# Attention inputs loaded ahead of weights, and two groups of heads side by side, in a fused attention and feed-forward kernel

## The chip, the cores and the metric

The kernel runs on one core of a Trainium2 chip. The time is the device time of one execution in microseconds (us); the profile of an execution gives its span, from the first to the last instruction. The engines are TensorE (PE, matmuls; PEld is its weight loads), VectorE (DVE), ScalarE (ACT) and GpSimd (POOL); SyncE (SP) issues most loads, POOL issues the others. Engines work in parallel, each through its own queue in order, and wait for one another through semaphores.

## The reference

```python
def sm_attn(qq, kk, vv):
    s = scale * np.matmul(qq, kk.transpose(0, 1, 3, 2))
    a = np.exp(s - np.max(s, axis=-1, keepdims=True))
    a = a / (np.sum(a, axis=-1, keepdims=True) + 1e-09)
    return np.matmul(a, vv)
p_packed = sm_attn(p, k, v)              # 32 packed queries against 576 keys
attn = sm_attn(q, p_packed, p_packed)    # 576 queries against the 32
x = attn.transpose(0, 2, 1, 3).reshape(8 * 576, 512)
h = x @ w_in                             # first feed-forward, 512 to 2048
x = (h * (1.0 / (1.0 + np.exp(-1.702 * h)))) @ w_out
h = np.maximum(np.maximum(x @ w1, x @ w2), x @ w3)   # second, 512 to 768
out = h @ w_out2
```

There are 8 batches of 8 heads, 576 tokens each, head size 64. The weights come as float64, the other inputs as float32.

## The kernel before

**Tiles and stages.** Attention works in 16 groups: a batch `b` and one of its two groups `g` of four heads. A group is a list of steps: `load_pk` (step 0), `load_v` (step 2) and `load_q` (step 7) issue its loads; `split_pk` builds a block-diagonal `pbd` from the packed queries; then s1 (packed queries times keys, `s`), a maximum (DVE), an exponential (ACT), transposes of the exponentials (`t` and `t1r`, copied to `et` by ACT), the product with v (`pv`), its masked and scaled copy (`pn`, DVE), its transpose (`ptp`, kept as `pt` and as a new `pbd`), s2 (queries times packed keys, also `s`), a softmax on DVE and ACT in the transposed layout (`a`), and `at`, the transposed probabilities, split by ACT and POOL.

The first feed-forward is folded with it: `pw` is packed value times `w_in`, so that `h` is `at` times `pw`. It goes chunk by chunk of 128 of the 2048 columns: `h_unit` (for two halves of 288 tokens), `g_unit` (the gate: `t` and `g`, on ACT, DVE, sometimes POOL) and `out_unit` (`acc`, with `w_out`). A product of two fp32 matrices is three matmuls of high and low parts (`mm3`). The second feed-forward follows from about 900 us on.

**Weights.** `w_in` and `w_out` arrive as the bits of float64. A piece of 1 MB (`raw_wi` or `raw_wo`, two loads of 512 KB on the SP queue) is turned into a high and a low part by `conv`: for the first four pieces by `convert`, six DVE instructions and two on ACT; for later ones by `convert_low`, which loads a second, shifted copy (`low_wi`, `low_wo`). Both piece kinds are named by quarter `n` of the 2048 columns: wi_0 is the pair for quarter 0. Converted `w_in` pieces are also saved to memory (`wsc`, by `wi_save`, 1 MB each, issued from POOL) for use by later batches.

**Order.** `main` makes a list of (due time, function) with `add`; the list is sorted by due time and traced in that order. The due times are plan numbers in us, not measured times. `attention(t, b, g, stretch)` gives step k of a group the time t plus its offset times `stretch`; `conv(t, ..., load, ...)` issues the loads `load` before t and the parts of the conversion at t and after it; `tn[n]` is the time of chunk n and starts at `T0`. The framework then orders each engine's queue, which runs strictly in that order. The SP queue has at most eight loads in flight: the ninth is issued when the first has landed.

Of the kernel before, what the change touches and what calls it, by code (L numbers as in the profile page):

```python
# [8 lines left out]
F32 = mybir.dt.float32  # L9
# [4 lines left out]
ALU = mybir.AluOpType  # L14
AX = mybir.AxisListType

B, H, S, D, NP = 8, 8, 576, 64, 32
DM, DFF, DFF2 = 512, 2048, 768
NT = B * S
P = 128  # L20
TB = 512
# [6 lines left out]
KD = DM // P  # L28
NQ = DFF // TB
SCALE = 1.0 / D ** 0.5  # L30
D_ = [-2, -8, 2.9, -2.51, 2.83, -0.47, -3.58, -0.6, 0.92, -0.32, -6.66, 0.91, 2.97, 2.32, -5.59, -0.32]
W_ = [60, 15.02, 42.09, 0]
K_ = [2, 11, -8, 6, 1, -7, 10, 6, -11, -14, -9, -5, -2, -13, -1, 4]
L_ = [8.18, 16.49, 4, 22.39]
Z_ = [1, 1, 1, 0, 0, 0, 0, 0, 0, 0, 0, 0, 0, 0, 0, 0]
PL_ = [10, 12]
Q_ = [12, 9, 9, 8]
# [5 lines left out]
def tile_packed_attention_moe(  # L43
# [13 lines left out]
    nc = tc.nc  # L57
# [5 lines left out]
    def stage_pool(name, bufs, side):  # L63
        return tc.alloc_tile_pool(name=name, bufs=bufs, side=side, reuse_waits="tile")
# [4 lines left out]
    ap_ = stage_pool("ap", 1, "right")  # L69
# [7 lines left out]
    def f(t):  # L77
        return t.bitcast(F32)
# [8 lines left out]
    def ur_tile(name):  # L87
        return urp.tile([P, S], F32, tag="ur", name=name)

    def u_tile(name, dt=F32):  # L90
        return up.tile([P, S], dt, tag="u", name=name)

    def x_tile(name, dt=F32):
        return up.tile([P, 4 * HALF], dt, tag="x", bufs=4, name=name)
# [24 lines left out]
    wsc = dram.tile([2, NQ, 2, P, 2, TB], F32R, name="wsc")  # L119

    wsa = dram.tile([9, P, 2, 2, 3, P], F32R, name="wsa")
    wss = dram.tile([9, P, 2, 2, 4, P], F32R, name="wss")


    def split(raw, hi, lo):
        nc.scalar.copy(hi, raw)  # L126
        nc.gpsimd.tensor_tensor(out=lo, in0=raw, in1=f(hi), op=ALU.subtract)  # L127

    def evac(o, hi, lo):
        nc.scalar.copy(hi, o)  # L130
# [67 lines left out]
    class Group:  # L198
# [2 lines left out]

        def load_pk(self):
            b, g = self.b, self.g
            self.praw = ap_.tile([P, 2, NP], F32, tag="praw", name=f"praw_{self.n}")
            nc.sync.dma_start(self.praw, p[b, g])
            self.kraw = self.load_t(k, "k")

# [33 lines left out]
        def split_t(self, raws, name):  # L241
            t = []
            for c in range(2):
                hl = [u_tile(f"{name}{x}_{self.n}_{c}", F32R) for x in range(2)]
                split(raws[c], *hl)
                t.append(hl)
            return t

        def load_v(self):
            self.vraw = []  # L250
            for c in range(3):
                raw = (u_tile if self.b < 2 else ur_tile)(f"raw_v_{self.n}_{c}")
                if c < 2:
                    nc.sync.dma_start(raw[:, :TB], v[self.b, self.g, :, c])
                else:
                    nc.sync.dma_start(raw[D:, :2 * P], vr[self.b, self.g])
                self.vraw.append(raw)

        def split_v(self):
            if self.b < 2:  # L260
                return
            self.v = []
            for c in range(3):
                if c < 2:
                    hl = [u_tile(f"v{x}_{self.n}_{c}", F32R) for x in range(2)]
                    split(self.vraw[c][:, :TB], *(t[:, :TB] for t in hl))
                else:
                    t = u_tile(f"v_{self.n}_{c}", F32R)
                    hl = [t[:, :2 * P], t[:, 2 * P:4 * P]]
                    split(self.vraw[c][D:, :2 * P], *(t[D:] for t in hl))  # L270
                self.v.append(hl)
# [205 lines left out]

    wo = {}
    gt, acc = {}, {}
    latest = {}  # L480

# [25 lines left out]
    start = {}  # L509
# [88 lines left out]
    class Piece:  # L598
# [12 lines left out]
        def conv(self):  # L611
            self.hl = [c_tile(f"wa{y}_{self.n}") for y in range(2)]
            self.v, self.s = conv_late(self.n, self.raw, *self.hl, TB)
# [211 lines left out]
    def add(t, fn, *a):  # L825
        plan.append((t, len(plan), fn, a))
# [27 lines left out]

    tpt, tend = {}, [0.0]

    def attention(t, b, g, stretch, dq=0.0):
        ts = []
        for k, (dt, fn) in enumerate(Group(b, g).steps()):
            after = {9: 7, 13: 12, 12: 11, 11: 10, 10: 8, 8: 6, 6: 5, 5: 3, 3: 1, 4: 2, 1: 0}.get(k)  # L860
            tk = t + dt * stretch + (D_[k] if b == 0 else 0) + (dq if k in (7, 9, 11, 12, 13) else 0)
            ts.append(tk if after is None else max(tk, ts[after] + .05))
            add(ts[-1], fn)
        tpt[b, g] = ts[10] + .05
        tend[0] = max(tend[0], ts[-1])

    def main():
        HU = 2.2
        T0 = 39

        attention(0.0, 0, 0, 1.07)
        attention(8, 0, 1, 1.07)
        attention(20, 1, 0, 0.97, 0)
        attention(34, 1, 1, 0.97, 0)

        N1 = 2 * B * NFC
        tn = [0.0] * 300
        t = T0
        for n in range(N1 + 2):
# [10 lines left out]
        sv = {}  # L890

        def wi_save(g, n):
            nc.gpsimd.dma_start(f(wsc[g, n].rearrange("c p a b -> p c a b")), f(sv[g, n]))

        def wi_store(g, n):
            def s(ws):
                sv[g, n] = ws
                if W_[n] == 0:
                    wi_save(g, n)
                for c in range(2):  # L900
                    wi[0, 2 * g + c, n] = ws[:, c]
            return s

        def wo_store(fc):
            def s(ws):
                wo[fc], wo[fc + 1] = (ws[:, x] for x in range(2))
            return s

        kk = 0
        for n in range(NQ):  # L910
            def tc_(kk):
                base = 7 + 6.49 * kk if n == 0 else tn[start[0, n]] - 22 + 7 * (kk - 4 * n)
                return base + K_[kk]
            for g in range(2):
                t = tc_(kk)
                conv(t, f"wi{g}_{n}", [w_in[2 * g, n], w_in[2 * g + 1, n]], wi_store(g, n), L_[kk] if kk < 4 else 19, Z_[kk], 0.0, 0 if kk < 4 else 10)
                if W_[n] > 0:
                    add(t + W_[n], wi_save, g, n)
                kk += 1
                for b in range(2):  # L920
                    add(max(t + .1, tn[start[b, n]] - PL_[b], tpt[b, g]), pw1_unit, b, g, n)
            for fc in range(4 * n, 4 * n + 4, 2):
                conv(tc_(kk), f"wo{fc}", [w_out[fc], w_out[fc + 1]], wo_store(fc), L_[kk] if kk < 4 else 19, Z_[kk], 0.0, 0 if kk < 4 else 10)
                kk += 1
# [37 lines left out]
        for idx in range(18):  # L962
            pc = Piece(idx // 2, idx % 2)
            t = TP + idx * TP_[1] if idx < 14 else TB0 - 10 + (idx - 14) * 10.5
# [5 lines left out]
        for fc in range(NF2):  # L970
            t = max(TP + 14 * TP_[1] + TP_[2] * fc, tn[225])
# [37 lines left out]
    if True:  # L1009
        main()  # L1010
        for _, _, fn, a in sorted(plan, key=lambda s: s[:2]):
            fn(*a)
        late["f"].release()
        late["x"].release()
        spp.release()
# [53 lines left out]
```

## Time and profile before

| | before |
|---|---|
| median of 3 runs | 1369.72 us |
| runs | 1369.72, 1370.19, 1366.59 us |
| the profiled execution | 1368.55 us, of which the span is 1366.8 us |
| TensorE busy | 1329.2 us, 97% of the span |
| VectorE busy | 974.7 us, 71% |
| ScalarE busy | 579.4 us, 42% |
| GpSimd busy | 248.2 us, 18% |
| mean granted TensorE clock | 0.992 of full speed |

Busy shares are means over the whole span. The change is in the first 60 us, where the first attention groups run, the first weights are loaded and no feed-forward chunk can start yet, so the windows of that stretch are to be read apart from the mean.

### The profile page before, as it was taken

The numbers are of one execution on the slowest core, as the hardware profiler recorded it, in microseconds if no ns is written. First come the engines' busy times: TensorE is split into PE (matmuls) and PEld (weight loads), VectorE is DVE, ScalarE is ACT, GpSimd is POOL, SyncE is SP. The second block draws the span as 40 slices with busy tenths as digits, with TensorE's granted clock in tenths as the row PEclk, the third lists the DMA queues.
The fourth block names the chain that finished last, engine by engine and source line by source line (L and its number), as shares of the span: only waits on it lengthen the run. The fifth ranks groups of instructions, "written<-read, shape, count | busy, mean of one in ns | idle before, by whom it ended". The sixth has DMA issues, their size and how long they took to land.

```text
span 1366.8 us, 22474 instructions
## 1 busy us (share of the span) xinstructions
PE 1329.2 (97%) x8450; PEld 1268.0 (93%) x8450; DVE 974.7 (71%) x1932; ACT 579.4 (42%) x1212; POOL 248.2 (18%) x342
## 2 busy tenths in 40 slices
PE   6799999999999999999999999999999999999998
PEld 3589889999999989999999999989999899899997
DVE  6899977877667576759999988746736557366461
ACT  3556655564554555555655652221311312223111
POOL 1120344424431034421000001101101011010000
PEclk7999999999999999999999999999999999999999
DMA  8669633552342324135756539947747567576451
GB/s 309 223 243 374 239 110 103 181 165 67 112 125 80 98 68 127 51 95 173 230 174 210 182 99 353 335 162 254 248 169 263 199 216 247 168 250 213 159 188 47
DMA packets 91691, 249.70 MB, mean 183 GB/s; under 512 B 10944, under 2 KB 40128, under 8 KB 84672
## 3 DMA queue, kind: packets, MB, share of 16 engines
q0 software_dynamic: 24640, 132.66, 28.5%
q1 hardware_dynamic: 66944, 115.62, 25.2%
q8 instruction: 66, 1.08, 0.3%
q14 instruction: 41, 0.34, 0.1%
HBM read 204.47 MB, written 43.78 MB: 182 GB/s over the span
## 4 chain that ended last, share of the span: by engine, by line
PE 83%; DVE 10%; DMA 3%; ACT 2%; issue 1%; SPq 0%; POOL 0%; ACTq 0%; DVEq 0%; POOLq 0%
PE p L103 10%; PE p L104 10%; PE p L102 10%; PE acc L102 8%; PE acc L104 8%; PE acc L103 8%; PE h L102 4%; PE h L104 4%; PE h L103 4%; PE accb L104 4%; PE accb L103 4%; PE accb L102 4%; DVE pw L131 1%; DMA low_wi<-in_w_in 1%; DVE t L524 1%
## 5 line engine op out<-in xcount | busy, mean ns | idle before, releaser
L102 PE MATMUL acc<-g,wo 128*128 128x288 f32 x1024 | 303.9, 299 | 1.8 <-DVE x L557 1.3
L103 PE MATMUL acc<-g,wo 128*128 128x288 f32 x1024 | 300.1, 293 | 1.5 <-DVE g L531 1.3
L104 PE MATMUL acc<-g,wo 128*128 128x288 f32 x1024 | 300.7, 294 | 0.0
L102 PEld LDWEIGHTS acc<-g,wo 128*128 128x128 f32 x1024 | 191.9, 188 | 7.0 <-DVE x L557 2.4
L103 PEld LDWEIGHTS acc<-g,wo 128*128 128x128 f32 x1024 | 192.7, 188 | 4.6 <-DVE g L531 2.2
L104 PEld LDWEIGHTS acc<-g,wo 128*128 128x128 f32 x1024 | 192.4, 188 | 0.7 <-issue 0.3
L531 DVE TENSOR_TENSOR g<-t,g 128x288 fp32r<-128x288 f32 x254 | 137.2, 540 | 42.0 <-ACT g L529 38.7
L529 ACT CAST g<-t 128x288 fp32r<-128x288 f32 x256 | 110.9, 433 | 118.3 <-DVE t L524 116.8
L523 ACT ACTIVATE t<-h 128x288 f32<-128x288 f32 x256 | 104.9, 411 | 122.9 <-PE h L104 121.5
L102 PE MATMUL h<-at,pw 128*128 128x288 f32 x512 | 153.2, 300 | 3.1 <-ACT at L126 1.7
L103 PE MATMUL h<-at,pw 128*128 128x288 f32 x512 | 151.6, 296 | 0.9 <-POOL at L127 0.9
L104 PE MATMUL h<-at,pw 128*128 128x288 f32 x512 | 151.2, 295 | 0.0
L524 DVE SCALAR_TENSOR_TENSOR t<-t,h 128x288 f32<-128x288 f32 x256 | 114.7, 449 | 51.0 <-ACT t L523 48.6
L658 POOL DMA_DIRECT2D wa<-wsa x54 | 28.6, 530 | 555.1 <-PE p L104 413.3
L744 DVE TENSOR_TENSOR u<-s,p 128x384 f32<-128x384 f32 x54 | 29.9, 554 | 119.4 <-PE p L104 119.4
L102 PE MATMUL p<-x_T,ws 128*128 128x384 f32 x324 | 108.2, 334 | 0.0
L103 PE MATMUL p<-x_T,ws 128*128 128x384 f32 x324 | 108.2, 334 | 0.0
L104 PE MATMUL p<-x_T,ws 128*128 128x384 f32 x324 | 108.1, 334 | 0.0
L102 PEld LDWEIGHTS h<-at,pw 128*128 128x128 f32 x512 | 96.0, 188 | 5.3 <-ACT at L126 2.0
L103 PEld LDWEIGHTS h<-at,pw 128*128 128x128 f32 x512 | 96.1, 188 | 1.4 <-POOL at L127 1.1
L104 PEld LDWEIGHTS h<-at,pw 128*128 128x128 f32 x512 | 96.1, 188 | 0.2
L774 ACT COPY s<-p 128x384 f32<-128x384 f32 x54 | 26.0, 481 | 161.8 <-PE p L104 161.6
(200 smaller groups left out, 3070.0 us busy)
## 6 DMA issues: line engine op xcount, KB each, us to landing
ws<-wss POOLq DMA_DIRECT2D x54, 1024.0 KB, 7.3
wa<-wsa POOLq DMA_DIRECT2D x54, 768.0 KB, 4.6
wi<-wsc POOLq DMA_DIRECT2D x48, 512.0 KB, 4.3
raw_k<-in_k SPq DMA_DIRECT2D x32, 288.0 KB, 3.1
raw_q<-in_q SPq DMA_DIRECT2D x32, 288.0 KB, 3.0
x2d<-x SPq DMA_DIRECT2D x16, 576.0 KB, 3.9
wss<-ws SPq DMA_DIRECT2D x36, 256.0 KB, 4.0
xr<-x2d SPq DMA_DIRECT2D x24, 384.0 KB, 4.4
```

The costliest lines, as they stand in the source:

```text
L102: nc.tensor.matmul(o, al, bh, start=start, stop=False, skip_group_check=more)
L103: nc.tensor.matmul(o, ah, bl, start=False, stop=False, skip_group_check=more)
L104: nc.tensor.matmul(o, ah, bh, start=False, stop=stop, skip_group_check=more)
L131: nc.vector.tensor_tensor(out=lo, in0=o, in1=f(hi), op=ALU.subtract)
L523: nc.scalar.activation(t, o, AF.Tanh, scale=0.5 * 1.702)
L524: nc.vector.scalar_tensor_tensor(out=t, in0=t, scalar=1.0, in1=o, op0=ALU.add, op1=ALU.mult)
L529: latest["act"] = nc.scalar.copy(g[:, 0], gt[n])
L531: latest["dve"] = eng.tensor_tensor(out=g[:, 1], in0=gt[n], in1=f(g[:, 0]), op=ALU.subtract)
L658: nc.gpsimd.dma_start(a, wsa[n % 9].rearrange("p i h b f -> p (i h b f)"))
L744: latest["dve"] = nc.vector.tensor_tensor(out=o, in0=a, in1=b, op=op)
L774: latest["act"] = nc.scalar.copy(self.s1, self.b1)
```

## The change

Loads of the first two batches get due times of their own (the new argument `loads`): those of batch 0 are due from -9 to -4, ahead of all weights, whose loads are then due from -4.5 on (11 less 15.5) in the order of the plan. The two groups of batch 0 are put 4.2 instead of 8 apart and those of batch 1 11 instead of 14 apart; the table `D_` of offsets by step goes; `T0`, the due time of the first chunk, goes from 39 to 33; the first four conversions are due at 11, 17.5, 24 and 30.5 instead of 9, 24.5, 11.98 and 32.47. `praw` has two buffers, so that the second group's is loaded without waiting for the first group's. For `b < 2` two chunks of v share one tile. `wi_save` is traced inside `tc.issue_after`, which puts the save behind the POOL instruction that `split` recorded last. No computation is added or removed.

```diff
-L_ = [8.18, 16.49, 4, 22.39]
+L_ = [15.5, 19, 23, 27]
...
     def split(raw, hi, lo):
         nc.scalar.copy(hi, raw)
-        nc.gpsimd.tensor_tensor(out=lo, in0=raw, in1=f(hi), op=ALU.subtract)
+        latest["pool"] = nc.gpsimd.tensor_tensor(out=lo, in0=raw, in1=f(hi), op=ALU.subtract)
...
-            self.praw = ap_.tile([P, 2, NP], F32, tag="praw", name=f"praw_{self.n}")
+            self.praw = ap_.tile([P, 2, NP], F32, tag="praw", bufs=2, name=f"praw_{self.n}")
...
+            if self.b < 2:
+                x = x_tile(f"raw_v_{self.n}")
             for c in range(3):
-                raw = (u_tile if self.b < 2 else ur_tile)(f"raw_v_{self.n}_{c}")
+                if self.b < 2:
+                    raw = x[:, c * TB:c * TB + TB] if c < 2 else u_tile(f"raw_v_{self.n}_{c}")
+                else:
+                    raw = ur_tile(f"raw_v_{self.n}_{c}")
...
-    def attention(t, b, g, stretch, dq=0.0):
+    def attention(t, b, g, stretch, dq=0.0, loads=None):
...
-            tk = t + dt * stretch + (D_[k] if b == 0 else 0) + (dq if k in (7, 9, 11, 12, 13) else 0)
+            tk = t + dt * stretch + (dq if k in (7, 9, 11, 12, 13) else 0)
+            if loads and k in (0, 2, 7):
+                tk = loads[(0, 2, 7).index(k)]
...
-        T0 = 39
-
-        attention(0.0, 0, 0, 1.07)
-        attention(8, 0, 1, 1.07)
-        attention(20, 1, 0, 0.97, 0)
-        attention(34, 1, 1, 0.97, 0)
+        T0 = 33
+
+        attention(0.0, 0, 0, 0.92, 0, (-9, -7, -5))
+        attention(4.2, 0, 1, 0.92, 0, (-8, -6, -4))
+        attention(18, 1, 0, 0.97, 0, (4, 11, 19))
+        attention(29, 1, 1, 0.97, 0, (12, 20, 27))
...
         def wi_save(g, n):
-            nc.gpsimd.dma_start(f(wsc[g, n].rearrange("c p a b -> p c a b")), f(sv[g, n]))
+            with tc.issue_after(latest["pool"].ins):
+                nc.gpsimd.dma_start(f(wsc[g, n].rearrange("c p a b -> p c a b")), f(sv[g, n]))
...
             def tc_(kk):
-                base = 7 + 6.49 * kk if n == 0 else tn[start[0, n]] - 22 + 7 * (kk - 4 * n)
-                return base + K_[kk]
+                if n == 0:
+                    return 11 + 6.5 * kk
+                return tn[start[0, n]] - 22 + 7 * (kk - 4 * n) + K_[kk]
```

**The load queue (SP).** Before, the first weight pair stood behind the first group's keys; the names give input, group and chunk.

```order
L205 DMA praw_0_106<-in_p 128x64
L238 DMA raw_k_0_0_108<-in_k 128x576
L238 DMA raw_k_0_1_110<-in_k 128x576
L139 DMA raw_wi_0_116<-in_w_in 128x1024 x2
L238 DMA raw_k_1_0_136<-in_k 128x576
L238 DMA raw_k_1_1_138<-in_k 128x576
L139 DMA raw_wo_150<-in_w_out 128x1024
L205 DMA praw_1_134<-in_p 128x64
L139 DMA raw_wo_150<-in_w_out 128x1024
L139 DMA raw_wi_0_153<-in_w_in 128x1024 x2
L238 DMA raw_k_0_0_245<-in_k 128x576
```

After the change, from the second group's packed queries on:

```order
L239 DMA raw_k_0_1_110<-in_k 128x576
L206 DMA praw_1_112<-in_p 128x64
L239 DMA raw_k_1_0_114<-in_k 128x576
L239 DMA raw_k_1_1_116<-in_k 128x576
L260 DMA raw_v_0_118<-in_v 128x512 x2
L262 DMA raw_v_0_2_121<-in_vr 64x256
L260 DMA raw_v_1_123<-in_v 128x512 x2
L262 DMA raw_v_1_2_126<-in_vr 64x256
L239 DMA raw_q_0_0_128<-in_q 128x576
L239 DMA raw_q_0_1_130<-in_q 128x576
L140 DMA raw_wi_0_132<-in_w_in 128x1024 x2
L239 DMA raw_q_1_0_135<-in_q 128x576
```

All of p, k and v of both groups and the first group's q now stand ahead of wi_0, and the first pair of `w_out` stands behind the second `w_in` pair.

**VectorE at the first conversion.** Before, `L176` to `L187` are the conversion of wi_0, `L300` the maxima of s1, `L304` to `L316` small steps on them:

```order
L300 TENSOR_REDUCE st_0_0_122<-s_0_0_0_119 128x1
L176 TENSOR_SCALAR tmp_wi_0_156<-raw_wi_0_116 128x1024
L179 TENSOR_SCALAR tmp_wi_0_156<-raw_wi_0_116 128x1024
L300 TENSOR_REDUCE st_0_0_122<-s_0_0_1_124 128x1
L180 SCALAR_TENSOR_TENSOR tmp_wi_0_156<-raw_wi_0_116,tmp_wi_0_156 128x1024
L304 TENSOR_SCALAR st_0_0_122<-st_0_0_122 128x1
L182 SCALAR_TENSOR_TENSOR tmp_wi_0_156<-raw_wi_0_116,tmp_wi_0_156 128x1024
L215 COPY pbd_1_140<-praw_1_134 64x2x32
L313 TENSOR_SCALAR st_0_0_122<-st_0_0_122 128x1
L215 COPY pbd_1_140<-praw_1_134 64x2x32
L186 TENSOR_SCALAR raw_wi_0_116<-tmp_wi_0_156 128x1024
L316 RECIPROCAL st_0_0_122<-st_0_0_122 128x1
```

After the change (line numbers are up to six higher: `L177` to `L188` the conversion, `L306` the maxima):

```order
L322 RECIPROCAL st_0_0_161<-st_0_0_161 128x1
L177 TENSOR_SCALAR tmp_wi_0_207<-raw_wi_0_132 128x1024
L306 TENSOR_REDUCE st_0_1_187<-s_0_1_0_184 128x1
L180 TENSOR_SCALAR tmp_wi_0_207<-raw_wi_0_132 128x1024
L306 TENSOR_REDUCE st_0_1_187<-s_0_1_1_189 128x1
L181 SCALAR_TENSOR_TENSOR tmp_wi_0_207<-raw_wi_0_132,tmp_wi_0_207 128x1024
L310 TENSOR_SCALAR st_0_1_187<-st_0_1_187 128x1
L183 SCALAR_TENSOR_TENSOR tmp_wi_0_207<-raw_wi_0_132,tmp_wi_0_207 128x1024
L319 TENSOR_SCALAR st_0_1_187<-st_0_1_187 128x1
L187 TENSOR_SCALAR raw_wi_0_132<-tmp_wi_0_207 128x1024
L322 RECIPROCAL st_0_1_187<-st_0_1_187 128x1
L177 TENSOR_SCALAR tmp_wi_0_269<-raw_wi_0_139 128x1024
```

The conversion of wi_0 moved behind the first group's maxima, and the second group's maxima stand between its parts; the `L177` row is the first of this queue that waits for a weight.

**GpSimd and its saves.** `L893` (after: `L901`) rows are the 1 MB saves; `L127` (after: `L128`) rows are splits, `at_0_0` those of the first group of batch 0, `at_1_1` the last of batch 1.

```order
L893 DMA wsc<-wi_0_157 128x2x1024
L211 MEMSET pbd_0_262 128x256
L893 DMA wsc<-wi_0_288 128x2x1024
L127 TENSOR_TENSOR at_0_0_319<-at_0_316,at_0_0_318 128x576
L127 TENSOR_TENSOR at_0_1_408<-at_1_405,at_0_1_407 128x576
L211 MEMSET pbd_1_411 128x256
L531 TENSOR_TENSOR g_459<-t_441,g_459 128x288
L531 TENSOR_TENSOR g_482<-t_479,g_482 128x288
L127 TENSOR_TENSOR at_1_0_495<-at_0_492,at_1_0_494 128x576
L893 DMA wsc<-wi_1_731 128x2x1024
L127 TENSOR_TENSOR at_1_1_703<-at_1_700,at_1_1_702 128x576
L893 DMA wsc<-wi_1_739 128x2x1024
```

After the change, from the same first split on:

```order
L128 TENSOR_TENSOR at_0_0_319<-at_0_316,at_0_0_318 128x576
L128 TENSOR_TENSOR at_0_1_375<-at_1_372,at_0_1_374 128x576
L212 MEMSET pbd_1_410 128x256
L536 TENSOR_TENSOR g_431<-t_428,g_431 128x288
L536 TENSOR_TENSOR g_478<-t_475,g_478 128x288
L128 TENSOR_TENSOR at_1_0_537<-at_0_534,at_1_0_536 128x576
L128 TENSOR_TENSOR at_1_1_709<-at_1_706,at_1_1_708 128x576
L901 DMA wsc<-wi_1_727 128x2x1024
L901 DMA wsc<-wi_1_735 128x2x1024
L901 DMA wsc<-wi_0_208 128x2x1024
L901 DMA wsc<-wi_0_270 128x2x1024
L220 MEMSET pbd_0_1443 128x576
```

The two saves of quarter 0 (`wi_0`) moved from ahead of all splits to behind `at_1_1`, where four saves now stand in a row. Further on in this queue the two saves of quarter 2, which before stood behind the splits of `k_2_0_1`, moved behind those of `k_3_0_1`.

## Rows read from the trace of the kernel before

**Rows 1.** The page: busy time and share of TensorE and VectorE.

```profile
PE 1329.2 (97%) x8450; PEld 1268.0 (93%) x8450; DVE 974.7 (71%) x1932; ACT 579.4 (42%) x1212; POOL 248.2 (18%) x342
PEclk7999999999999999999999999999999999999999
```

**Rows 2.** Windows by stage: length, busy time of each engine, granted clock, DMA share, GB/s.

```profile
0.00:14.50 14.50, 5.96 (x14) 3.72 (x15) 7.07 (x15) 5.61 (x10) 2.07 (x14) 0.89 0.87 324
14.50:31.00 16.50, 11.92 (x30) 7.39 (x29) 11.86 (x19) 6.96 (x12) 1.19 (x2) 0.60 0.93 343
31.00:57.27 26.27, 19.77 (x84) 13.70 (x82) 21.53 (x41) 11.59 (x23) 3.81 (x4) 0.98 0.63 221
57.27:82.00 24.73, 24.18 (x148) 21.55 (x149) 21.31 (x46) 14.96 (x32) 3.77 (x4) 1.00 0.77 294
82.00:122.10 40.10, 38.24 (x263) 36.05 (x262) 38.48 (x66) 23.90 (x47) 7.04 (x6) 1.00 0.70 255
122.10:178.00 55.90, 49.86 (x352) 47.39 (x350) 51.94 (x95) 33.96 (x62) 15.63 (x15) 1.00 0.75 276
178.00:1366.80 1188.80, 1179.21 (x7567) 1138.18 (x7567) 822.50 (x1657) 482.37 (x1029) 214.67 (x297) 1.00 0.51 169
```

**Rows 3.** Timeline of VectorE: start, length, instruction, idle time before it and releaser.

```profile
8.27 0.69 DVE L176 TENSOR_SCALAR tmp_wi<-raw_wi 128x1024 int32<-128x1024 int32 x1 [1.40 <-DMA raw_wi<-in_w_in]
...
24.62 0.48 DVE L356 SCALAR_TENSOR_TENSOR pn<-pv,st,mask 128x256 f32<-128x256 f32 x1 [0.92 <-PE pv L347]
...
52.36 0.78 DVE L425 STREAM_TRANSPOSE at<-a 128x576 f32<-128x576 f32 x1
...
55.70 0.39 DVE L215 COPY pbd<-praw 64x64 f32<-64x64 f32 x2 [1.65 <-POOL pbd L211]
...
57.27 0.45 DVE L524 SCALAR_TENSOR_TENSOR t<-t,h 128x288 f32<-128x288 f32 x1
...
140.43 0.70 DVE L158 TENSOR_SCALAR low_wi<-low_wi 128x1024 int32<-128x1024 int32 x1 [1.22 <-DMA low_wi<-in_w_in]
```

**Rows 4.** Chain of work that ended last, 0 to 75 and 120 to 180 us.

```profile
5.75 7.87 DMA raw_wi<-in_w_in
...
122.73 17.61 DMA low_wi<-in_w_in
```

**Rows 5.** Windows of TensorE alone: length, busy time, granted clock, DMA share, GB/s.

```profile
11.30:18.20 6.90, 5.56 (x13) 0.51 1.04 391
18.20:21.60 3.40, 1.00 (x5) 1.00 1.03 407
21.60:31.80 10.20, 8.05 (x21) 0.50 0.78 282
```

**Rows 6.** Window of VectorE, only instructions with a wi_0 temporary: length, busy time.

```profile
0.00:14.50 14.50, 5.39 (x6) 0.89 0.87 324
```

**Rows 7.** Timeline of TensorE: start, length, instruction, idle before it.

```profile
20.59 3.99 PE L347 MATMUL pv<-raw_v,et 128*128 128x256 f32 x10 [2.43 <-ACT e L309]
...
28.72 3.73 PE L389 MATMUL s<-raw_q,pbd 128*128 128x288 f32 x8 [0.75 <-ACT pbd L370]
...
40.40 2.21 PE L389 MATMUL s<-raw_q,pbd 128*128 128x288 f32 x8 [1.96 <-ACT e L309]
...
48.52 2.62 PE L347 MATMUL pv<-raw_v,et 128*128 128x256 f32 x10 [0.16 <-ACT et L328]
```

**Rows 8.** VectorE groups of 53.30 to 57.27 us: count, busy time, mean ns.

```profile
L160 DVE SCALAR_TENSOR_TENSOR raw_wi<-raw_wi 128x1024 int32<-128x1024 int32 x1 | 1.2, 1226 | 0.0
L155 DVE TENSOR_SCALAR raw_wi<-raw_wi 128x1024 int32<-128x1024 int32 x1 | 0.7, 675 | 0.0
```

**Rows 9.** Loads of raw_wo issued at 120.7 to 121.8 us: starts, and time to landing.

```profile
L139 SPq DMA_DIRECT2D raw_wo<-in_w_out x2: 440/593/746, 120.8 to 121.3; - x2
...
DMA to landing us min/median/max: 13.8/14.8/15.9
```

**Rows 10.** Saves wsc issued at 120 to 123.5 us: time to landing.

```profile
DMA to landing us min/median/max: 11.1/12.8/14.5
```

More of the change, by code (lines that the diff above doesn't have):

```diff
@@ L30 @@
 SCALE = 1.0 / D ** 0.5
-D_ = [-2, -8, 2.9, -2.51, 2.83, -0.47, -3.58, -0.6, 0.92, -0.32, -6.66, 0.91, 2.97, 2.32, -5.59, -0.32]
 W_ = [60, 15.02, 42.09, 0]
 K_ = [2, 11, -8, 6, 1, -7, 10, 6, -11, -14, -9, -5, -2, -13, -1, 4]
-L_ = [8.18, 16.49, 4, 22.39]
+L_ = [15.5, 19, 23, 27]
 Z_ = [1, 1, 1, 0, 0, 0, 0, 0, 0, 0, 0, 0, 0, 0, 0, 0]
@@ L122, in tile_packed_attention_moe @@
     wss = dram.tile([9, P, 2, 2, 4, P], F32R, name="wss")
+    latest = {}
     def split(raw, hi, lo):
         nc.scalar.copy(hi, raw)
-        nc.gpsimd.tensor_tensor(out=lo, in0=raw, in1=f(hi), op=ALU.subtract)
+        latest["pool"] = nc.gpsimd.tensor_tensor(out=lo, in0=raw, in1=f(hi), op=ALU.subtract)
     def evac(o, hi, lo):
@@ L479, in tile_packed_attention_moe @@
     gt, acc = {}, {}
-    latest = {}
     PAT = {
```

## The prediction

> **What bounds the kernel now.** The page comes first: TensorE is busy 97% of the span, VectorE 71%, and the granted clock is below full only in the first of the forty slices [rows 1]. So nothing in the middle can give much, and the start is to be read apart. The windows by stage [rows 2] give VectorE's idle time: 14.50 less 7.07 is 7.43 us by 14.5, then 4.64 by 31.0, then 4.74 by 57.27, together 16.81 beside 40.46 of work. TensorE idles more there (8.54, 4.58, 6.50). From 57.27 to 82 TensorE is full (24.18 of 24.73; VectorE has 3.42 of slack), from 82 to 122 VectorE is (38.48 of 40.10), from 122 to 178 VectorE has 3.96 idle, and from 178 on TensorE works 1179.21 of 1188.80. Time saved at the start therefore stays saved if neither engine owes more work later.
>
> In the timeline of VectorE the reader is to see how the start hangs together [rows 3]: the first weight conversion at 8.27 after a wait for its load, the first group's `pn` at 24.62, the second group's `at` at 52.36, a wait of 1.65 for POOL's zeroed `pbd`, and at 57.27 the gate's first product `t`, behind which TensorE goes on without long gaps. The chain of waits [rows 4] shows weights and q loads at the start (a load of wi_1 issued at 5.75 lands 7.87 later, at 13.62), and at 122.73 a `low_wi` load that takes 17.61.
>
> Last, TensorE's windows [rows 5]: it works at a granted clock of 0.51 (the 1.2 GHz level), is at full from 18.2, falls back at 21.6 after a stretch with 1.00 of 3.40 us busy, and is at 0.50 until 31.8.
>
> **The change, part by part.**
>
> *Loads first.* wi_0 now follows 13 input loads. A 128x576 fp32 chunk is 288 KB, v of a group 576 KB, a weight pair 1024 KB. Ahead of wi_0's end stand two packed queries (64), k, v, k, v, q (2880) and itself: 3968 KB. Before, the first half of wi_1, landed at 13.62 [rows 4], ended 3776 KB (64, k of one group 576, wi_0 1024, k 576, wo 1024, half 512). The 192 KB more (0.2 MB) take 0.5 us at 391 GB/s [rows 5]: 14.1. More and smaller loads pass the eight places, so I take **14.5**, bounds 14.1 and 15.0. wi_1 follows after q and itself, 1600 KB or 1.64 MB at 0.39 to 0.41 MB per us: 18.5.
>
> *VectorE's first wait.* The order puts `L177` of wi_0 ahead of the second group's maxima. Until 14.5 VectorE then does only what is not conversion: 7.07 less 5.39 [rows 2, 6] is 1.7, and 2.2 with the overlap of neighbours. Idle: 12.3, not 7.43, a loss of 4.9. Queued behind the wait are those maxima; they would be ready by about 13 to 15, so the wait costs them little, and their exponential starts at 17.8.
>
> *Second stage.* From 14.5 VectorE runs through to about 21.6 (5.4 us of conversion [rows 6] and 1.7 of maxima and small steps, all data present). ACT gives `t1r` and `et` at 18.9, so `pv` of the first group starts at 18.9, not 20.59 [rows 7]. At full clock it takes 2.62, at half about 5 (the 3.99 of before ran 1.0 at full); at half but for the last bit I take 4.8: end 23.7, `pn` at 23.75 for 24.62 [rows 3]. VectorE waits 2.15 there and about 1 more for the second `pn` and the first `a`: idle 3.2 for 4.64. The second `pv` now stands ahead of s2, and the weights for filler lie ready.
>
> *Third stage.* From 31 on VectorE's waits before were 4.74, of which 1.65 was POOL's `pbd` [rows 3], which now is traced elsewhere; the others were waits on exponentials and `pn` where no conversion was left to fill. Now wo_0 and wo_2, conversions of the plan's 24 and 30.5, lie there. I take 0.7; bounds 0 and 4.7.
>
> *Sum of the start.* Idle 12.3 + 3.2 + 0.7 = 16.2 for 16.81. The new order reaches the first `t` before two instructions of wi_1's second pair (`L155` 0.68, `L160` 1.23 [rows 8]), which before stood ahead: work 40.46 less 1.9 = 38.6. So `t` comes at 54.8 or so, 2.5 earlier, but VectorE owes 1.9. TensorE has the same work left and goes on after one more `pbd` copy, about 1.7 earlier than before. The debt of 1.9 fits the slack of 3.42 up to 82; if it does not, only 0.6 remains. **Term: -1.7**, bounds 0 and -2.8 (all of the second stage at full clock).
>
> *Late saves.* Two saves of 1 MB leave the start, where DMA share was 0.87 and 0.93 [rows 2]; I count no gain for it. Four now go out together at about 84; their 4 MB take some 11 us at 390 GB/s, beside the `low` loads due then. Before, two went out around there. What that costs a load is seen at 120 to 137, where two saves of quarter 2 were out for 11.1 to 14.5 us [rows 10]: two 512 KB loads issued 0.5 apart landed 2.6 apart [rows 9] instead of the 1.3 that 0.4 MB per us gives, so a pair of loads comes some 2.6 later. I take 0 at 84, since VectorE has conversions at hand there (38.48 of 40.10 busy), and 3 as the bound of the loss. The saves of quarter 2 leave 120 to 137. Without their 2 MB the `low_wi` load of 17.61 [rows 4] ends up to 5 earlier, and VectorE's wait for it, 1.22 [rows 3] of the 3.96 idle there [rows 2], goes. **Term: -1.1**, bounds 0 and -1.2.
>
> The page "DMA: Bandwidth & Descriptors" of the Trainium skill, section "SWDGE vs HWDGE vs iDMA", says that an engine takes turns between the software and the hardware queue. Rows 9 agree (2.6 for 1.3). It speaks against the four bunched saves near 84: by it every load beside them takes twice as long, and the sum would be 1368.8, at C below.
>
> *`praw`, shared v tile.* Nothing is computed more; the tiles are free at the start. Cost 0, covered by loads that land before use (v of both groups is ahead of wi_0's 14.5, and the first `pv` is at 18.9).
>
> Sum: -1.7 - 1.1 = **-2.8** on the profiled 1368.55 us (span 1366.8 and 1.75 around it), which stands 1.2 under the median of 1369.72 and near the mean of the three runs. 1368.55 - 2.8 = 1365.8.
>
> **The rivals.** A measurement of this kernel tells some 0.3% from no change, 4.1 us; the two bounds are 1364.4 and 1372.7.
>
> *A, the forecast:* 1365.8, own range 1364.4 to 1368.
>
> *B, TensorE stays at full clock from the first `pv` on.* The two groups side by side leave TensorE fewer gaps. The first `pv` then takes 2.62 instead of 4.8 (-2.2) and the first s2 2.21 instead of 3.73 [rows 7] (-1.5), of which VectorE's own work covers 0.4: -3.3 more, 1362.5. For it: the clock was full from 18.2 to 21.6 [rows 5], just where `pv` now starts. Against: it fell there with 1.00 us busy of 3.40.
>
> *C, the change does nothing measurable.* VectorE's 4.9 us of lost early work comes back as debt, the wait at 140 is replaced by loads beside the bunched saves: 1368.5.
>
> *D, slower: half clock through the whole start.* Before, the clock was full from 31.8 on. TensorE now idles longer at once: no `pv` and no s2 can run between the s1 of the second group, done by 15, and 18.9. If the clock stays at 1.2 GHz until the first `h`, the second `pv` costs 2.6 more and the two s2 1.5 more each (3.73 for 2.21 [rows 7]): 5.6. All of TensorE's 19.77 us from 31 to 57.27 [rows 2] would take 39.5, 13.3 more than that window. Of these ends I take 7.5, near the lower, since the other matmuls there have VectorE's chain beside them: 1368.55 + 7.5 - 2.8 = 1373.3. It decides from a loss of 6.9 on, that is if nearly all of the stretch to 46 us stays slow. For it: two falls of the clock before [rows 5]. Against: as many matmuls stand in fewer microseconds.
>
> The Trainium skill, "TensorE: Matmul & The Clock Gate", section "HAM oscillation — how this bites in real kernels", tells of a kernel in which every wait between short bursts of matmuls sends the clock back to half; rows 5 show the same twice, and it is D's rule.
>
> **How the numbers follow.** A 0.42, B 0.36, C 0.12, D 0.10. Faster is B alone, 0.36; same is A and C, 0.54; slower is D, 0.10. The predicted time is A's. The range takes in A and C, most of B (its time less 1 for the bound of the start, 1361.5) and, on the other side, the bound of 3 lost at 84 us with no gain elsewhere, 1371.0: it leaves out most of D and the fast end of B, some 0.2. The forecast's own range is 1364.4 to 1368.
>
> **What would show it right or wrong.** In the profile after: `L177` at 14.1 to 15.0 with a wait of 5 us or so for `raw_wi`; the first `pn` near 23.75; VectorE's idle time to its first `t` near 16, and that `t` at 54 to 56; the granted clock in 18 to 32 us, which tells A from B and D; no wait for `low_wi` near 140; four saves together near 84 and how late the loads beside them land. The prediction is wrong if the first `t` comes later than 57, if VectorE's idle time by 31 us is above 17, or if a wait for a load appears between 82 and 122.

## The result and the profile after

The changed kernel takes 1375.64 us (median of 10 runs, 1373.8 to 1378.36), the kernel before 1369.02 in the same measurements: ratio 1.0053, 95% interval 1.004 to 1.0065. That is 6.6 us slower, above the range of the prediction (1361.5 to 1371.0), which had put 0.10 on slower, by another mechanism.

The page of the changed kernel, beside [rows 1]:

```profile
span 1373.7 us, 22457 instructions
PE 1334.1 (97%) x8450; PEld 1273.1 (93%) x8450; DVE 974.9 (71%) x1932; ACT 579.4 (42%) x1212; POOL 248.2 (18%) x342
```

The counts of matmuls and weight loads are the same; TensorE's busy time grew by 5, which fits time at a lower clock (shown below). The windows of [rows 2], now with one from 820 to 850 us (length, busy time of the five engines, granted clock, DMA share, GB/s):

```profile
0.00:14.50 14.50, 8.66 (x20) 5.46 (x20) 2.46 (x9) 3.25 (x7) 2.32 (x15) 1.00 0.83 269
14.50:31.00 16.50, 10.00 (x34) 6.74 (x35) 12.05 (x20) 7.22 (x13) 0.00 (x0) 0.79 1.04 384
31.00:57.27 26.27, 19.39 (x67) 13.11 (x66) 25.40 (x44) 12.69 (x24) 3.56 (x3) 0.82 0.47 169
...
820.00:850.00 30.00, 26.36 (x141) 26.04 (x141) 20.73 (x49) 5.04 (x11) 4.34 (x8) 0.89 0.87 293
```

VectorE idles 12.04, 4.45 and 0.87 us in the first three, 17.4 in all, where the prediction had 12.3, 3.2 and 0.7. So VectorE's idle time at the start is close to what was worked out, and in this execution the start is not where the time is lost. VectorE's timeline shows both places:

```profile
16.38 0.69 DVE L177 TENSOR_SCALAR tmp_wi<-raw_wi 128x1024 int32<-128x1024 int32 x1 [5.70 <-DMA raw_wi<-in_w_in]
...
24.96 0.48 DVE L362 SCALAR_TENSOR_TENSOR pn<-pv,st,mask 128x256 f32<-128x256 f32 x1 [1.55 <-PE pv L353]
...
51.27 0.77 DVE L431 STREAM_TRANSPOSE at<-a 128x576 f32<-128x576 f32 x1
...
57.03 0.44 DVE L529 SCALAR_TENSOR_TENSOR t<-t,h 128x288 f32<-128x288 f32 x1
...
836.48 0.56 DVE L749 TENSOR_TENSOR m<-u,p 128x384 f32<-128x384 f32 x1 [7.36 <-DMA x2d<-x]
```

The first `t` comes at 57.03 for 57.27 [rows 3]. The last row is new: 780 us later, in the first block of the second feed-forward (which begins near 820 us, not 900), VectorE stands for 7.36 us before it writes its second `m` tile, and what releases it is `x2d<-x`, a store of the first feed-forward's output to memory. In the kernel before, the same `m` waited for TensorE alone, and TensorE was full at the full clock; VectorE's timeline and the window from 820 to 850 us of that kernel:

```profile
830.44 0.55 DVE L744 TENSOR_TENSOR m<-u,p 128x384 f32<-128x384 f32 x1 [1.58 <-PE p L104]
```

```profile
820.00:850.00 30.00, 30.00 (x180) 30.00 (x179) 26.57 (x62) 8.15 (x16) 5.28 (x10) 1.00 1.02 361
```

In the changed kernel TensorE is 99% busy from 178 to 818 us, as before; its timeline and its windows (length, busy time, clock, DMA share, GB/s) show what follows:

```profile
837.09 0.69 PE L101 MATMUL p<-x_T,ws 128*128 128x384 f32 x1 [3.65 <-DVE m L749]
```

```profile
825.00:830.00 5.00, 5.00 (x31) 1.00 0.98 340
830.00:835.00 5.00, 3.45 (x20) 1.00 1.07 402
835.00:840.00 5.00, 2.91 (x9) 0.62 1.10 364
840.00:845.00 5.00, 5.00 (x23) 0.69 0.41 152
```

TensorE waits 3.65 us for `m`, and after that idle stretch it runs at the 1.2 GHz level to about 843, which costs the other 3 of the 6.7 us lost here. The same store in the kernel before (issued at 824.8) took as long, and nothing waited for it; the time from issue to landing, of before and then of the changed kernel:

```profile
DMA to landing us min/median/max: 11.2/11.2/11.2
```

```profile
L568 SPq DMA_DIRECT2D x2d<-x x1: 777/777/777, 825.0 to 825.0; - x1
...
who waited for it (us, times):
  DVE m L749: 7.4, 1
...
DMA to landing us min/median/max: 11.4/11.4/11.4
```

**Why `m` waits for it.** The pool `up` holds two kinds of tiles, 18 `u` and 4 `x`, and the kind that is requested first lies first in memory. Before, the first request was a `u` tile; now `load_v` requests an `x` tile (its new shared v tile) ahead of any `u`. In the compiled programs the `x` buffers moved from bytes 185632 to 204063 of each partition to 144160 to 162591. When `up` and `gp` are released, the second feed-forward's pool takes over their memory. That `m` tile lies at 152224 to 153759 in both programs; the `x2` tile that the last store reads lay at 190240 to 194847 before and lies at 148768 to 153375 now. So that `m` may not be written before the store is done. Nothing in the queues' order shows this; it is a wait on memory, 780 us behind the edit.

### The profile page after: what moved, and what is told of

It reads as the page before. It is cut to its first block, busy times and chain, and to the rows that moved or that the text cites. A ratio compares the mean times of both kernels' runs of the same rounds, so it can differ in the third digit from the quotient of the medians.

```text
span 1373.7 us, 22457 instructions
## 1 busy us (share of the span) xinstructions
PE 1334.1 (97%) x8450; PEld 1273.1 (93%) x8450; DVE 974.9 (71%) x1932; ACT 579.4 (42%) x1212; POOL 248.2 (18%) x342
## 4 chain that ended last, share of the span: by engine, by line
PE 82%; DVE 11%; DMA 3%; ACT 1%; issue 1%; SPq 1%; POOL 0%; DVEq 0%; ACTq 0%; POOLq 0%
PE p L101 9%; PE p L103 9%; PE p L102 9%; PE acc L101 8%; PE acc L102 7%; PE acc L103 7%; PE h L102 4%; PE h L101 4%; PE h L103 4%; PE accb L103 4%; PE accb L102 4%; PE accb L101 4%; DVE pw L132 1%; DVE g L536 1%; DVE t L529 1%
```

## The experiments

Theory L (layout) puts the loss on that wait; theory S (start) on the later weights and the clock of the first 60 us. In the traces the queues of all engines have the same rows in the same order in e1 as in the changed kernel, in e2 as in the kernel before, and in f7 as in e3 below: in these three pairs only addresses differ.

**e1: the `u` tile requested first.**

```diff
             if self.b < 2:
+                last = u_tile(f"raw_v_{self.n}_2")
                 x = x_tile(f"raw_v_{self.n}")
...
-                    raw = x[:, c * TB:c * TB + TB] if c < 2 else u_tile(f"raw_v_{self.n}_{c}")
+                    raw = x[:, c * TB:c * TB + TB] if c < 2 else last
```

> The changed kernel, with one thing moved: in load_v the u tile of the third v chunk is requested before the shared x tile, so that the u buffers lie ahead of the x buffers in memory, as in the kernel before. All queues keep the order of the changed kernel. Theory L (layout): of the 6.9 us that the changed kernel is slower in the profiles, 6.6 come between 811 and 843 us, where the first m of the second feed-forward shares memory with an x2 tile whose store to memory is still under way; the start itself gains or loses under 1 us. It expects that the wait of m for x2d is gone, no fall of the clock after 833, and 1368 to 1370 us, level with the kernel before (ratio 0.998 to 1.001). Theory S (start): the later weights and the clock at the start cost the time, and the wait near 833 only takes the place of another; it expects 1374 to 1376 us again.

Measured: 1372.19 us, ratio 1.0017 (1.0004 to 1.0031). The wait is gone, but only half of the loss in the median: neither theory's number. VectorE's `m` and the window from 820 to 850 us, as in the kernel before:

```profile
833.20 0.55 DVE L750 TENSOR_TENSOR m<-u,p 128x384 f32<-128x384 f32 x1 [1.63 <-PE p L103]
```

```profile
820.00:850.00 30.00, 30.00 (x185) 29.91 (x184) 26.61 (x60) 9.39 (x18) 5.29 (x10) 1.00 0.97 340
```

**e2: the kernel before with the `x` buffers first.**

```diff
+    for y in range(4):
+        x_tile(f"first_{y}")
```

> The kernel before, with the four x buffers requested (and not used) ahead of everything else, so that they lie ahead of the u buffers in memory; loads, order and code are otherwise those of the kernel before. Theory L: the first m now waits for the store of x2 near 833 us for some 4 us, the clock falls after it, and the time is 1375 to 1377 us (ratio 1.0045 to 1.0055), as slow as the changed kernel. Theory S: nothing at the start differs, so 1368 to 1370 us.

Measured: 1375.53 us, ratio 1.0044 (1.0029 to 1.006). Theory L, in its time and its place; VectorE's and TensorE's timelines of this kernel:

```profile
840.69 0.55 DVE L747 TENSOR_TENSOR m<-u,p 128x384 f32<-128x384 f32 x1 [7.38 <-DMA x2d<-x]
```

```profile
841.30 0.44 PE L105 MATMUL p<-x_T,ws 128*128 128x384 f32 x1 [3.67 <-DVE m L747]
```

**e3: e1, and saves without `issue_after`.**

```diff
-            with tc.issue_after(latest["pool"].ins):
-                nc.gpsimd.dma_start(...)
+            nc.gpsimd.dma_start(...)
```

> As e1, and wi_save without issue_after, so that the saves of quarter 0 go out at about 25 to 35 us and those of quarter 2 at about 120, as in the kernel before. My prediction's term for the late saves was a gain of 1.1 us, from a wait near 140 that goes: by it this is about 1 us slower than e1. The rival, that the four bunched saves near 90 cost what the others gain, expects it level with e1 or up to 2 us faster.

Measured: 1369.14 us, ratio 0.9999 (0.9986 to 1.0013), 3.0 below e1, where the prediction's term asks for 1 above it and the rival for at most 2 below. The intervals of the two still overlap; f7 below gives a second pair.

**e4: e1, and the first weight pair ahead of v.** `L_[0]` 18.5 for 15.5.

> As e1, and the load of the first weight pair put ahead of v of the first two groups, in place of behind q (L_[0] 18.5 for 15.5); no other row of any queue moves. If VectorE's wait for that weight, 5.70 us until 16.4, sets the start, the first conversion begins at 10 to 12, the first t of the gate comes 2 to 4 us earlier than in e1, and the time is 1 to 3 us below e1. If the start is set by TensorE's chain and its clock, or what is gained is given back later, the time is within 1 us of e1.

Measured: 1368.34 us, ratio 0.999 (0.9978 to 1.0001), 3.9 below e1. The conversion of wi_0 begins at 11.09, as expected. The first `t` comes at 57.8: 3.1 earlier than in e1's first profile (60.9), as expected too, but 1 later than in two further profiles of e1 (g1 and g2 below, 56.6 and 56.9) and later than in the changed kernel (57.0). So it is not shown that the gain came from VectorE's wait.

**f1: e1, e3 and e4 together.**

> The edits of e1 (u buffers first), e3 (saves without issue_after) and e4 (first weight pair ahead of v) together. e3 was 3.0 us below e1 and e4 3.9, each with an interval of some 2.5. If late saves and late weights are two separate costs, they add up: 1372.2 - 3.0 - 3.9 = 1365.3, 1364 to 1367, which is below the kernel before (ratio 0.996 to 0.999). If both only undo the same wait of VectorE between 82 and 178 us, the time is that of the better one, 1368 to 1369.

Measured: 1366.83 us against 1370.01 for the kernel before, ratio 0.998 (0.997 to 0.999): faster than both kernels, and inside the range of the sum (ratio 0.996 to 0.999), not at the time of the better one alone.

**f2: the kernel before with `issue_after` around `wi_save`.**

> The kernel before with one part of the change, issue_after around wi_save: the saves of quarter 0 go out behind at_1_1 at about 90 us together with those of quarter 1, those of quarter 2 at about 180. My prediction's term is a gain of 1.1 us (1367 to 1368). The theory from e1 and e3, that four saves in a row beside the loads at 90 to 110 us delay the conversions which VectorE has no slack for, expects a loss of 1.5 to 3.5 us: 1370.5 to 1372.5.

Measured: 1369.04 us, ratio 0.9996 (0.9987 to 1.0005). Late saves alone cost nothing that can be measured in the kernel before, so the theory made from e1 and e3 (a loss of 1.5 to 3.5) falls in that form; the prediction's gain of 1.1 lies inside the interval (-1.8 to 0.7 us) and is not shown either.

**f7: the changed kernel without `issue_after`.**

> The changed kernel without issue_after, x buffers still first: with e1, e3 and the changed kernel it makes a square of two parts (layout, saves). If layout costs 6 us with late saves and with early ones, as in e2 (6.6), it is 1375 to 1376. If the cost of layout is 3.5, the difference of the changed kernel and e1, it is 1372 to 1373. The wait of m for x2d near 833 us is expected in the trace either way.

Measured: 1372.88 us, ratio 1.0028 (1.0017 to 1.0039). Layout costs 2.9 thousandths with early saves and 3.6 with late ones, 4 to 5 us: the lower of the two numbers expected, and less than in each profile (table below); the times also hold the start, which differs from execution to execution. Late saves, with the queues that go with them, cost 2.5 thousandths with `x` first (the two intervals do not overlap) and 1.8 with `u` first. The wait is there:

```profile
839.94 0.55 DVE L749 TENSOR_TENSOR m<-u,p 128x384 f32<-128x384 f32 x1 [7.49 <-DMA x2d<-x]
```

**g1, g2, g3: further profiles of e1 and of the changed kernel.** One profiled execution each.

> The kernel of e1 once more, one profiled execution. Its twelve times spread from 1368.6 to 1374.6, and its first profile had TensorE at the 1.2 GHz level through most of 14.5 to 31 us and was 4.2 us behind the kernel before at 113 us, where the changed kernel, with the same queues, was level with it. Theory C (clock): the start of this kernel comes out in two ways from execution to execution, by where the clock falls; a further profile is either level with the kernel before at 113 us (within 1 us, 1368 to 1370 us in all) or 3 to 5 us behind. Rival: the other addresses of the v tiles make the start of e1 slower each time, so 4 us behind again. No wait of m for x2d in either.

> As the run before it, a third profile of e1: by theory C level with the kernel before at 113 us in at least one of the two; by the rival 3 to 5 us behind in both.

> The changed kernel once more, one profiled execution. The wait of m for the x2d store near 833 us and the fall of the clock behind it are there again, 5.4 to 6.3 us between 811 and 845 us, whatever the start is like; 1374 to 1379 us.

Measured: 1368.97, 1368.79 and 1380.5 us, beside 1366.61 for the kernel before on that chip (one run). Both profiles of e1 are level with the kernel before at 113 us (-0.5 and -0.2), as theory C has it; its rival, a start that is slower each time, falls. g3 has the wait again (7.61 us), but missed its numbers: above 1379 us, and 6.9 us lost between 811 and 845 for 5.4 to 6.3. TensorE's first 31 us in the first profile of the changed kernel and in its second (g3), timeline and one window:

```profile
10.77 3.52 PE L293 MATMUL s<-raw_k,pbd 128*128 128x288 f32 x8
...
20.82 4.11 PE L353 MATMUL pv<-raw_v,et 128*128 128x256 f32 x10
...
26.92 2.62 PE L353 MATMUL pv<-raw_v,et 128*128 128x256 f32 x10 [0.35 <-ACT et L342]
```

```profile
10.56 2.11 PE L293 MATMUL s<-raw_k,pbd 128*128 128x288 f32 x8
...
20.31 4.93 PE L353 MATMUL pv<-raw_v,et 128*128 128x256 f32 x10
...
27.84 4.76 PE L353 MATMUL pv<-raw_v,et 128*128 128x256 f32 x10 [0.35 <-ACT et L342]
```

```profile
18.20:31.00 12.80, 10.51 (x26) 0.50 1.04 385
```

Same program, same order, two starts. Where s1 of the second group ran fast (2.11 us, 406 ns for a matmul), TensorE then waited 7.16 us (the idle time before the next row, `t1r`) and was at 1.2 GHz for all of 18 to 31; where it ran slower (3.52, 687 ns for most of the matmuls), it waited 6.05 and the clock was back at full by the second `pv` (2.62 for 4.76). (The windows give 1.00 for 10.5 to 12.5 us in both profiles, so they do not tell the two apart there.) e1 has both starts too: its first profile is of the slow start (0.50 from 18.2 to 31), g1 and g2 are of the other (0.79). Its twelve times fall apart in the same way: the seven executions with a mean granted clock of 0.987 to 0.989 (the first profile has 0.989) took 1371.60 to 1374.63 us, the five at 0.991 (g2 has 0.991, g1 0.993) 1368.59 to 1371.14. So what is left of the loss in e1's median goes, as far as this shows, with the slower start; why one execution takes it and another doesn't is not shown.

The table follows one matmul in three places (records 1049, 5500 and 5640 of the 8450 on TensorE, in order of their starts; before at 201.63, 818.12 and 840.99 us), as its start less that of before:

| profile | at 202 us | at 818 | at 841 | between the last two |
|---|---|---|---|---|
| changed | -0.21 | 0.25 | 6.93 | 6.7 |
| changed again (g3) | 4.68 | 5.00 | 11.94 | 6.9 |
| e2, before with x first | 3.51 | 4.44 | 9.99 | 5.6 |
| f7 | 5.46 | 3.59 | 10.14 | 6.6 |
| e1 | 4.18 | 2.71 | 2.76 | 0.1 |
| e1 again (g1) | -0.59 | 0.25 | 0.25 | 0.0 |
| e1, third (g2) | -0.42 | 0.03 | 0.04 | 0.0 |
| e3 | -1.07 | -1.29 | -1.28 | 0.0 |
| f2, before with late saves | 0.61 | 1.20 | 1.33 | 0.1 |
| e4 | 1.45 | 1.92 | 1.92 | 0.0 |
| f1 | -0.84 | -1.00 | -0.68 | 0.3 |

Layout costs 5.6 to 6.9 us in each of the four profiles with `x` first, and 0.0 to 0.3 in the seven others, whatever the start was. With the changed kernel's queues the start is worth -0.6 to 4.7 us by the execution (five profiles). It is not the change alone that does this: e2, with the queues of the kernel before, is 3.5 behind that kernel's one profile at 202 us, and its first `pv` took 4.93 for 3.99 [rows 7].

## Why the prediction was wrong

**The step that failed** is "`praw`, shared v tile. Nothing is computed more; the tiles are free at the start. Cost 0". The tiles are free at the start; the cost comes from where the other tiles then lie. No rival had it: D ended on the slow side by the clock of the start. That mechanism is real (g3 is 4.7 us behind at 202 us), but it isn't the cause here: the changed kernel's first profile was level with the kernel before at 202 us and 6.9 behind at the end. Of the prediction's own signs the first `t` just passed its limit of 57 (57.03; 61.3 in g3), VectorE's idle time by 31 us stayed under 17 (16.5), and no wait for a load appeared between 82 and 122: they all look at the first 122 us, and the loss lay at 833.

**Loads first: mis-sized.** wi_0 was forecast at 14.5 and its conversion began at 16.38. The rate was taken from a stretch at 391 GB/s; the windows of the changed kernel's early loads:

```profile
4.90:10.50 5.60, 4.18 (x11) 2.48 (x10) 1.63 (x6) 1.07 (x4) 0.00 (x0) 1.00 0.93 295
10.50:12.50 2.00, 2.00 (x6) 1.57 (x6) 0.16 (x1) 0.58 (x1) 0.00 (x0) 1.00 1.06 330
12.50:16.30 3.80, 1.79 (x5) 0.91 (x4) 0.00 (x0) 0.00 (x0) 0.00 (x0) 1.00 1.03 403
```

k, v and the first of q moved at 295 to 330 GB/s with the DMA engines about as busy as later at 403, where the rest of q and the weights move. Why is not shown.

**Second and third stage: mechanism right, size off by that.** The first `pv` started at 20.82 for 18.9 and `pn` came at 24.96 for 23.75, 1.9 and 1.2 late, where the load was 1.9 late. Up to the first `t` (57.03 for 54.8) VectorE idled 17.4 us for 16.2 and worked 39.7 for 38.6: of the 1.9 of work that was to move behind that `t`, only 0.8 did. So the lead of 1.7 was 0.2 at 202 us, in the better of the two starts, and of the whole forecast gain of 2.8 nothing was left at 818 (0.25 behind).

**Late saves: the sign was wrong in the changed kernel** (e1 beside e3, the changed kernel beside f7), and in the kernel before it is open (f2). VectorE's wait for `low_wi` near 140 did go. The wait for `low_wo` stayed (2.58 for 2.01), and its price in TensorE was not in the sum, since before had it too: TensorE waits behind it at about 178 for 2.68 in the kernel before, 3.13 in the changed one. The waits of TensorE at that place in e1 and in e3:

```profile
PE s L101 <- DVE a L406: 3.1, 1, 3.1
```

```profile
PE s L101 <- DVE a L406: 0.4, 1, 0.4
```

In e3 and f7 VectorE's queue is also ordered otherwise from about 36 us on and TensorE's from about 42 (the framework ordered them anew without the edge), with that `low_wo` instruction one place further back. So the 3.0 us between e1 and e3 are not shown to be the saves' traffic; the f2 run speaks against it. What part is order, what part traffic, and what part the starts of the runs, stays open.

**Two rules.** The store of 576 KB took 11.4 us, and 11.2 before, beside loads issued from GpSimd: from 826 to 836.4 us GpSimd's queue (software) moved 2.75 MB in 430 packets and SyncE's (hardware) 1.11 MB in 814. The Trainium skill states in "DMA: Bandwidth & Descriptors", section "SWDGE vs HWDGE vs iDMA", that a DMA engine takes turns between the queues of the two kinds. The runs do not show such turns apart from the rest of the traffic. The clock was at half behind the wait near 833 (3 of the 6.7 us) and, in the slower of the two starts, from 18 to 31 us, around a wait of 7.16. The Trainium skill, "TensorE: Matmul & The Clock Gate", section "HAM oscillation — how this bites in real kernels", tells of waits between stretches of matmuls that send the clock back to half; both places agree.

## What to carry to other kernels

A tile requested from a pool in a new order can move every buffer of that pool, as it did here, and a pool that later takes the memory over inherits other waits: after such an edit look at the addresses, or look in the trace for a wait on a DMA that nobody waited for before, over the whole span and not only around the edit. Compare two traces by the start of the same matmul along the span; the place of a loss can then be read off. A late store that is harmless while nobody needs its tile's memory costs its wait, and here also the clock behind it. And where one program has two starts, one profile of each kernel is not enough to compare them.

## What the runs showed of the hardware

A wait of 3.65 us in a full TensorE cost 6.7, since the clock fell to the lower level behind it (0.62 and 0.69 in two windows of 5 us). One program had starts that differ by 4 to 5 us from execution to execution, after a fast (2.11 us) or a slow (3.36 to 3.52 us) run of the same eight matmuls: in the five profiles with the changed kernel's queues the fast one was followed by the slower start. It is no sign in itself: in e3 and f7, alike in their queues, the fast one (2.11) came before the start with the clock back at full (0.77 from 18.2 to 31 us) and the slow one (3.36) before the start at half (0.50). And the share of busy DMA engines did not show the rate: 1.06 at 330 GB/s, 1.03 at 403.
